# Wo's loads, a K halo and sums of h in another order, and two more groups whose MLP runs all 18 pairs of W2 rows in seven products

## The chip, the cores and the metric

The kernel runs on one core of a Trainium2 chip. The metric is the device time of one execution, in microseconds (us). A core has the engines PE (TensorE: matmuls, and weight loads beside them), DVE (VectorE), ACT (ScalarE), POOL (GpSimd) and SP (SyncE, which here only issues DMAs). Each engine runs its own instructions in order and waits on semaphores for the others. DMA queues move data between DRAM and the core's memory.

## The reference, cut to what matters

One transformer block on 2048 tokens with D = 576, 32 heads of 18, and an MLP width F = 4608. Attention is local and dilated: each token looks at 8 positions, itself and every second one before it.

```python
def _A_ref(x, wqkv, wo):                       # H=32, Dh=18, W=8, dil=2
    q, k, v = split(x @ wqkv)
    idx = pos[:, None] - arange(W)[None, :] * dil          # masked where negative
    logits = einsum("bhsd,bhswd->bhsw", q, k[:, :, idx]) * Dh ** -0.5
    o = einsum("bhsw,bhswd->bhsd", softmax(logits), v[:, :, idx])
    return o.reshape(B, S, D) @ wo

def _B_ref(x, w1, b1, w2, b2):
    h = _gelu(einsum("bsd,df->bsf", _layernorm(x), w1) + b1)
    return einsum("bsf,fd->bsd", h, w2) + b2

h  = x + _A_ref(_layernorm(x), A_wqkv, A_wo)
h2 = h + _B_ref(_layernorm(h), B_w1, B_b1, B_w2, B_b2)
```

## The kernel before

**Tiling.** The 2048 tokens are 16 tiles of 128 rows (one row of each 16 neighbours, so that tile j - 2 holds the neighbours that tile j looks at). x, q and the K and V of eight tiles (`kv_ring`, one ring for even and one for odd tiles) stay on the core. The weights are loaded once: Wo in four slices (`load_wo`, two DMAs each, line 104), W1 in six, W2 in seven. W2 has 36 row tiles of 128 rows, taken as 18 pairs of an even and an odd one.

**Order.** Every engine's instruction order is written by hand. First come 24 visits of q, k and v products (PE, line 222), each with work in the tables `between` and `after` and with weight loads in `loads`, all keyed by the number of the visit. The normalized x goes through DRAM and comes back transposed (`out_x` lines 284 and 285, `in_x` line 288, both issued by SP). The attention and second layer norm of the first two tiles are in these visits too.

Then a loop over 8 groups of two tiles. In iteration k PE does the first MLP product of group k (324 matmuls), the Wo products of group k + 1 (36 matmuls, `wo_visit`), and the second MLP product of group k. Beside it DVE does the attention logits of group k + 2 (`att_qk_a` line 344, `att_qk_b` lines 353 to 364, `att_max` lines 368 and 369), the softmax denominators and probabilities (`att_den`, lines 395 to 397), the weighted sums of V (lines 401 to 408), the residual `ln2_h` (line 467) and its statistics. ACT does the gelu (line 578), the exponentials and the normalizations; POOL does the inverse roots (lines 161 and 492) and the accumulating DMAs `accumulate_h` and `out_sum` (line 787).

**Queues around the change.** SP issues in order: the attention output goes to DRAM (`send_o`, lines 204 and 205, tile `td`) and is read back transposed (`read_o`, line 439, tile `oT`), which Wo's products of the next group use as weights. The normalized h goes the same way (`ln2_send`, then `ln2_in`, line 508, into the tile `hnT`, of which there is one buffer). The output stores are on SP too (line 790). A K or V halo (`halo`, line 339) reloads one ring slot behind the product that read it; its issue waits for that product. An issue that waits holds up all issues behind it on SP. `reload_x` (line 462) brings back x of a later group.

**The second MLP product.** Groups 0 and 1 run it plainly (line 597). From group 2 on, `mlp2_fast` takes two token tiles, the even and odd W2 rows and the two halves of the columns as a product of 2x2 blocks and computes it with seven block products in place of eight. For this DVE makes four sums of h for each pair of row tiles (`h_sums`, line 667) and four sums of W2 (`w2_sums`, line 657), the latter once. In the text of the sums S0 to S3 and T0 to T3 are the first index `t`. The sums of h of the first 12 pairs are made in operations of 128x1536, those of pairs 12 to 15 in 128x512, pairs 12 to 17 in 128x768. Groups 2 to 5 take 16 pairs in seven products and the last two pairs plainly (16 x 7 + 2 x 8 = 128 matmuls of 128x288), groups 6 and 7 take all 18 (126). `mlp2_fast` runs a list of steps: a pair (n, range) is product n, a name is a point at which the hooks of the loop are called ("hc", "h", "6", "7", "in", "exp", "4", "3"), or a step of its own.

Sums have no memory of their own; `s_slot` and `t_slot` place them in parts of `kv_ring`, `q_all` and `x_all` that are free at that time.

Of the kernel before, what the change touches and what calls it, by code (L numbers as in the profile page):

```python
# [11 lines left out]
BF16 = mybir.dt.bfloat16  # L12
F32 = mybir.dt.float32
F16 = mybir.dt.float16
# [3 lines left out]
def kernel(  # L18
# [13 lines left out]
    P = 128  # L32
# [6 lines left out]
    KT = 5  # L39
# [5 lines left out]
    HALF = D // 2  # L45
# [10 lines left out]
    GROUPS = [ATT_ORDER[i:i + 2] for i in range(0, NT, 2)]  # L56
# [551 lines left out]
    def ring_blocks(r, b0, n, size):  # L608
        flat = kv_ring[r][:].rearrange("p w t d -> p (w t d)").bitcast(F16)
        return flat[:, b0:b0 + n * size].rearrange("p (m c) -> p m c", c=size)  # L610
# [5 lines left out]
    def t_slot(t, m0, m1):  # L616
        if t == 2:
            return w2_block(0, 1, m0, m1).bitcast(F16)
        i = (0, 1, None, 2)[t]
        if m0 >= 16:  # L620
            return ring_blocks(1, (2 * i + m0 - 16) * HALF, m1 - m0, HALF)
        if i == 2 and m0 < 16:
            return ring_blocks(0, RING_T + m0 * HALF, m1 - m0, HALF)
        part = 0 if m1 <= 8 else 1 if m1 <= 12 else 2
        rows, j0 = ((x_all, (1, 9, 13)[part]), (q_all, (4, 12, 0)[part]))[i]
        m = m0 - (0, 8, 12)[part]
        j = j0 + 2 * (m // 2)
        if m1 - m0 > 2:
            return rows[:, j:j + m1 - m0 - 1:2, :].bitcast(F16).rearrange("p a (b c) -> p a b c", c=HALF)
        return rows[:, j, (m % 2) * HALF:(m % 2 + m1 - m0) * HALF].bitcast(F16).rearrange("p (b c) -> p b c", c=HALF)  # L630

    SR = 12
    ring1_free = [False]
    step_of = [0]
    RING_T = 3 * SR * P

    def s_slot(t, m0, m1):
        if t == 2:
            return h_block(0, 1, m0, m1)
        i = (0, 1, None, 2)[t]  # L640
        if m0 < SR:
            return ring_blocks(0, (i * SR + m0) * P, m1 - m0, P)
        if not ring1_free[0]:
            rows, j = ((q_all, 15), (x_all, 10), (x_all, 8))[i] if step_of[0] == 2 else (q_all, 15 - 2 * i)
            return rows[:, j, (m0 - SR) * P:(m1 - SR) * P].bitcast(F16).rearrange("p (m c) -> p m c", c=P)
        return ring_blocks(1, 6 * HALF + (i * (NM - SR) + m0 - SR) * P, m1 - m0, P)

    def h_block(odd, i, m0, m1):
        return h_all[:, 2 * m0 + odd:2 * m1:2, i * P:(i + 1) * P].bitcast(F16)
# [49 lines left out]
    def c_(fn, *a):  # L699
        return lambda: fn(*a)  # L700
# [2 lines left out]
        return ap.rearrange("p (g c) -> p g c", g=2)  # L703

    def mlp2_fast(g, rows, tags, wo, hooks):
        last, summed = wo is None, rows < NM
        q, p, r, s = tags
        j0, j1 = g
        af = psum_pair(q, "po")
        a, f = (af[:, n, 0:HALF] for n in range(2))  # L710
        b, d = psum_pair(p, "po")[:, 0, 0:HALF], None
        o0, o1 = (new_o(j, summed) for j in g)
        flat = kv_ring[1][:].rearrange("p w t d -> p (w t d)")
        rest = halves(flat[:, W * 2 * D - 2 * D:W * 2 * D].bitcast(F32))
        bank = {1: a, 2: a, 3: f, 4: b, 6: b}

        def add(out, x, y):
            nc.vector.tensor_tensor(out=out, in0=x, in1=y, op=ALU.add)

        def last_out():  # L720
            nc.vector.tensor_copy(out=o0[:, HALF:HALF + HALF // 2], in_=f[:, 0:HALF // 2])
            nc.scalar.copy(out=o0[:, HALF + HALF // 2:D], in_=f[:, HALF // 2:HALF])
            nc.sync.dma_start(out=out3[:, j0, HALF:D], in_=o0[:, HALF:D])

        def out0(n0, n1):
            if summed:
                nc.scalar.copy(out=halves(o0), in_=af[:, :, 0:HALF])
                return
            add(halves(o0)[:, n0:n1], af[:, n0:n1, 0:HALF], halves(x_of(j0))[:, n0:n1])
            nc.sync.dma_start(out=out3[:, j0, n0 * HALF:n1 * HALF], in_=o0[:, n0 * HALF:n1 * HALF])  # L730

        def out1():
            if summed:
                add(o1[:, HALF:D], bank[5], o1[:, 0:HALF])
                add(o1[:, 0:HALF], b, o1[:, 0:HALF])
                out_sum(j1)
                return
            add(o1[:, 0:HALF], b, rest[:, 0])
            add(o1[:, HALF:D], bank[5], rest[:, 1])
            nc.sync.dma_start(out=out3[:, j1, :], in_=o1)  # L740

        def do_rest():
            if summed:
                nc.scalar.copy(out=o1[:, 0:HALF], in_=bank[7])
                return
            add(rest, bank[7].unsqueeze(1).to_broadcast([P, 2, HALF]), halves(x_of(j1)))

        def take():
            bank[7], bank[5] = (psum_pair(tag, "po")[:, 0, 0:HALF] for tag in (r, s))

        lo, hi, all_ = (0, SR), (SR, rows), (0, rows)
        seed = {"b": (1, 6), "d": (6, 5), "f": (5, 3)}
        does = {
            "wo": lambda: wo((r, s)), "e": take, "rest": do_rest, "o1": out1,
            "o0": lambda: last_out() if last else out0(0, 2), "lo": lambda: out0(0, 1),
            "11": lambda: plain(0, 0, a, rows), "12": lambda: plain(0, 1, f, rows),
            "21": lambda: plain(1, 0, b, rows), "22": lambda: plain(1, 1, bank[5], rows),
        }
        if rows < NM:
            steps = ["wo", "hc", (1, all_), "b", "h", "e", (7, lo), (2, all_), (6, all_), "6", "7", "d", "11", (7, hi), "rest", "in",  # L760
                      (5, all_), "f", "exp", (4, all_), "21", "22", "o1", "4", (3, all_), "12", "o0", "3"]
        elif not last:
            steps = ["wo", "hc", (1, all_), "b", "h", "e", (7, lo), (6, all_), "6", "d", "7", (2, all_), (7, hi), "rest", "in",
                     (5, all_), "f", (4, all_), "o1", "4", (3, all_), "o0"]
        else:
            steps = ["e", (1, lo), (7, lo), (1, hi), "b", "h", (7, hi), "rest", (6, all_), "d", (2, all_), "lo",
                     (5, all_), "f", (4, all_), "o1", (3, all_), "o0"]
        for step in steps:
            if isinstance(step, tuple):
                product(step[0], bank[step[0]], *step[1])  # L770
            elif step == "f" and last:
                add(f, bank[5], x_of(j0)[:, HALF:D])
            elif step in seed:
                nc.scalar.copy(out=bank[seed[step][1]], in_=bank[seed[step][0]])
            else:
                call([does[step]] if step in does else hooks.get(step, ()))
# [22 lines left out]
    with tc.manual_schedule(engines={ENG.PE, ENG.Activation, ENG.DVE, ENG.SP, ENG.Pool}):  # L799
# [129 lines left out]
            ln2_ins(c, d)  # L929

        loads = {}
        for v, fns in ((2, [(load_w1, 0)]), (3, [(load_w1, 1)]), (4, [(load_w1, 2)]), (6, [(load_wo, [0])]), (8, [(load_wo, [1, 2])]),
                       (11, [(load_wo, [3])]), (14, [(load_w1, 4)]), (18, [(load_w1, 5), (load_w2, 0)]), (19, [(load_w2, 1)]),
                       (20, [(load_w2, 2)]), (21, [(load_w2, 3)]), (22, [(load_w2, 4)])):
            loads[v] = [c_(*fn) for fn in fns]
        after = {
# [87 lines left out]
        def wo_visit(*duos, fill=False):  # L1024
            visit([wo_duo(j, tag) for j, tag in duos], (lambda: [ahead[0]() for _ in range(2)]) if fill else None)

        FULL = (6, 7)
        p, q, r, s = "ABDC"

        gelu_table()  # L1030
        for k, g in enumerate(GROUPS):
# [38 lines left out]
            if 2 < k < 7:  # L1070
                m1[0] += [c_(pv_sum, c), c_(send_o, c), c_(pv_sum, d), c_(read_o, c), c_(send_o, d), c_(read_o, d)]
            if k < 6:
                m1[1] = m1.get(1, []) + [c_(att_qk_one, e, 0)]
                m1.setdefault(3, [])
                if k == 2:
                    m1[0] += [c_(pv_sum, d), c_(send_o, d), c_(read_o, d)]
                    m1[3] += [c_(w2_sums, 0, 8, (2, 3)), c_(w2_sums, 8, 12, (2, 3)), c_(w2_sums, 12, 14, (0, 1)), c_(w2_sums, 14, 16, (0, 1)),
                              c_(w2_sums, 12, 14, (2, 3)), c_(w2_sums, 14, 16, (2, 3))]
                m1[3] += [c_(h_sums, 0, SR, (0,))]
                x["hc"] += [c_(h_sums, 0, SR, (2,))]  # L1080
                x["h"] += [c_(h_sums, 0, SR, (1, 3)), c_(h_sums, SR, 16)]
                x["7"] += [c_(att_max, [e]), c_(att_qk_one, f, 1), c_(att_max, [f])]
                x["exp"] += [c_(exps, e, f)]
                x["4"] += [c_(att_den, e, f)]
            else:
                if k == 6:
                    ring1_free[0] = True
                    m1[1].append(c_(w2_sums, 16, NM))
                m1[3] = m1.get(3, []) + [c_(h_sums, 0, SR)]
                if k == 7:  # L1090
                    mid[3] = {1: [c_(h_sums, SR, 16)]}
                    x["h"] += [c_(h_sums, 16, NM)]
            if k + 3 < len(GROUPS):
                x["3" if k == 2 else "in"] += [c_(reload_x, GROUPS[k + 3])]
            wo = None
            if c is not None:
                if k == 6:
# [51 lines left out]
```

## Time and profile before

| what | value |
|---|---|
| median of 3 runs | 358.5 us (358.41 to 358.68) |
| the profiled execution | 358.75 us |
| its span | 357.0 us |
| granted TensorE clock | 1.00 |
| matmuls, busy time of PE | 4945, 351.1 us |
| busy time of DVE, ACT, POOL | 298.2, 235.9, 47.6 us |
| DMA moved | 46.29 MB |

How to read it: the profile gives one execution. The span runs from the first to the last instruction that it records; the profiled time holds 1.75 us more. A line of a timeline has the start, the duration, the engine ("SPq" is SP issuing DMAs), the line of the kernel, the operation with what it writes and reads, and in brackets how long the engine was idle before it and what ended that. A line of the chain of waits has start, duration, engine and what ran; each step is followed back to what released it. Matmul rows overlap, since matmuls are pipelined. A line of the queues has the packets, the megabytes and the share of the time of 16 DMA engines; q8 brings instructions.

### The profile page before, as it was taken

The numbers are of one execution on the slowest core, as the hardware profiler recorded it, in microseconds if no ns is written. First come the engines' busy times: TensorE is split into PE (matmuls) and PEld (weight loads), VectorE is DVE, ScalarE is ACT, GpSimd is POOL, SyncE is SP. The second block draws the span as 40 slices with busy tenths as digits, with TensorE's granted clock in tenths as the row PEclk, the third lists the DMA queues.
The fourth block names the chain that finished last, engine by engine and source line by source line (L and its number), as shares of the span: only waits on it lengthen the run. The fifth ranks groups of instructions, "written<-read, shape, count | busy, mean of one in ns | idle before, by whom it ended". The sixth has DMA issues, their size and how long they took to land.

```text
span 357.0 us, 11587 instructions
## 1 busy us (share of the span) xinstructions
PE 351.1 (98%) x4945; PEld 287.4 (81%) x4945; DVE 298.2 (84%) x428; ACT 235.9 (66%) x524; POOL 47.6 (13%) x63
## 2 busy tenths in 40 slices
PE   8999999999999999999999999999999999999996
PEld 4787778887788877887788778877887788778874
DVE  5999999999988999999998999999999998520431
ACT  4889767996647692678567856695669566606620
POOL 2340004000212010201200220022002200210000
PEclk9999999999999999999999999999999999999999
DMA  7997799954847574942553445345535353262001
GB/s 244 327 292 188 174 249 291 388 195 89 207 72 119 162 230 76 129 75 69 92 101 75 117 104 79 86 109 108 85 85 101 66 87 50 59 129 38 4 1 34
DMA packets 63492, 46.29 MB, mean 130 GB/s; under 512 B 32192, under 2 KB 61760, under 8 KB 63440
## 3 DMA queue, kind: packets, MB, share of 16 engines
q1 hardware_dynamic: 59472, 41.50, 44.1%
q0 software_dynamic: 3744, 3.84, 10.3%
q8 instruction: 38, 0.62, 0.7%
q10 hardware_dynamic: 224, 0.22, 0.2%
q14 instruction: 14, 0.11, 0.1%
HBM read 23.38 MB, written 12.42 MB: 100 GB/s over the span
## 4 chain that ended last, share of the span: by engine, by line
DVE 43%; PE 43%; DMA 6%; issue 3%; ACT 2%; SPq 2%; POOL 0%; DVEq 0%; POOLq 0%; ACTq 0%
PE po L687 21%; PE pm L222 19%; DVE prod L401 7%; DVE prod L353 7%; DVE prod L344 6%; DVE prod L407 5%; DVE ln_stats L148 3%; PE pw L222 2%; DMA kv_ring<-kv_dram 2%; DVE h L467 1%; DMA x_all<-in_A_x_dram 1%; DVE den L395 1%; ACT h_all L578 1%; DVE q_all L408 1%; DMA td<-q_all 1%
## 5 line engine op out<-in xcount | busy, mean ns | idle before, releaser
L222 PE MATMUL pm<-hnT,w_sb 64*128 64x256 bf16 x2304 | 142.9, 269 | 0.0
L578 ACT ACTIVATE h_all<-pm,b_sb 128x256 f16<-128x256 f32 (+1 forms) x288 | 108.5, 497 | 50.8 <-PE pm L222 50.2
L222 PEld LDWEIGHTS <-w_sb 64*128 64x128 bf16 x2304 | 111.6, 94 | 15.1 <-issue 1.7
L222 PE MATMUL pq<-wq_sb,xnT 64*128 64x288 bf16 x720 | 54.9, 283 | 1.2 <-DMA xnT<-xd 0.6
L687 PEld LDWEIGHTS <-h_all 128*128 128x128 f16 x464 | 44.8, 98 | 12.9 <-issue 1.4
L222 PEld LDWEIGHTS <-xnT 64*128 64x128 bf16 x864 | 41.9, 94 | 12.4 <-DMA xnT<-xd 0.9
L353 DVE TENSOR_TENSOR prod<-prod 128x2304 bf16<-128x2304 bf16 (+1 forms) x64 | 44.2, 691 | 2.1
L401 DVE TENSOR_TENSOR prod<-kv_ring,probs 128x4608 bf16<-128x4608 bf16 x16 | 40.9, 2558 | 1.9 <-DMA kv_ring<-kv_dram 1.4
L344 DVE TENSOR_TENSOR prod<-kv_ring,q_all 128x4608 bf16<-128x4608 bf16 x16 | 40.9, 2555 | 0.2
L222 PE MATMUL pm<-hnT,w1h_sb 64*128 64x256 bf16 x288 | 39.2, 269 | 0.0
L407 DVE TENSOR_TENSOR prod<-prod 128x2304 bf16<-128x2304 bf16 (+1 forms) x32 | 33.9, 1058 | 1.1
L597 PEld LDWEIGHTS <-h_all 128*128 128x128 bf16 x288 | 27.8, 98 | 8.0 <-issue 1.2
L687 PE MATMUL po<-w2a_sb,h_all 128*128 128x288 bf16 (+1 forms) x252 | 34.0, 286 | 0.0
L687 PEld LDWEIGHTS <-kv_ring 128*128 128x128 f16 x252 | 24.7, 98 | 6.2
L597 PE MATMUL po<-w2a_sb,h_all 128*128 128x288 bf16 x224 | 28.6, 286 | 0.0
L787 POOL DMA_DIRECT2D x_all<-o_sb x12 | 10.7, 889 | 126.4 <-PE pw L222 54.4
L222 PE MATMUL pq<-wqh_sb,xnT 64*128 64x288 bf16 x144 | 27.4, 283 | 0.0
L492 POOL TENSOR_TENSOR ln_rstd<-ln_var,mhalf 128x1 f32<-128x1 f32 x13 | 9.8, 758 | 77.7 <-ACT ln_var L491 77.7
L667 DVE TENSOR_TENSOR kv_ring<-h_all 128x1536 f16<-128x1536 f16 (+3 forms) x9 | 6.8, 754 | 15.7 <-ACT h_all L578 15.7
L222 PE MATMUL pw<-wo_sb,oT 64*128 64x288 bf16 x256 | 19.5, 283 | 0.1
L161 POOL TENSOR_TENSOR ln_rstd<-ln_veps,mhalf 128x1 f32<-128x1 f32 (+2 forms) x14 | 13.1, 947 | 44.3 <-PE o_pt L182 26.4
L687 PE MATMUL po<-w2b_sb,h_all 128*128 128x288 bf16 (+1 forms) x112 | 18.8, 286 | 0.1
(121 smaller groups left out, 409.3 us busy)
## 6 DMA issues: line engine op xcount, KB each, us to landing
w_sb<-in_B_w_dram SPq DMA_DIRECT2D x6, 768.0 KB, 7.7
kv_ring<-kv_dram SPq DMA_DIRECT2D x28, 144.0 KB, 2.3
kv_dram<-kv_ring SPq DMA_DIRECT2D x13, 288.0 KB, 3.3
w2a_sb<-in_B_w_dram SPq DMA_DIRECT2D x3, 1008.0 KB, 10.2
x_all<-in_B_b_dram SPq DMA_DIRECT2D x15, 144.0 KB, 4.1
td<-q_all SPq DMA_DIRECT2D x14, 144.0 KB, 1.8
td<-hn SPq DMA_DIRECT2D x14, 144.0 KB, 1.8
x_all<-h POOLq DMA_DIRECT2D x14, 144.0 KB, 4.8
```

Source lines behind the costliest of these rows:

```text
L148: nc.vector.bn_stats(out=stats[:, i, c, :], in_=src[:, c * HALF:(c + 1) * HALF])
L161: nc.gpsimd.tensor_tensor(out=rstd[:], in0=veps[:], in1=mhalf[:].to_broadcast([P, n]), op=ALU.pow)
L222: last = nc.tensor.matmul(duo["g"][r ^ swap][i], lhsT=lhsT, rhs=rhs, start=(swap == 0 and i == 0 and kt == 0), stop=(swap == 1 and kt == K ...
L344: ins = nc.vector.tensor_tensor(out=prod[:], in0=k_ring[j % 2], in1=q_all[:, j, :].unsqueeze(1) .to_broadcast([P, W, D]), op=ALU.mult).ins
L353: nc.vector.tensor_tensor(out=prod[:, :, o * H:o * H + n], in0=prod[:, :, a * H:a * H + n], in1=prod[:, :, c * H:c * H + n], op=ALU.add)
L401: nc.vector.tensor_tensor(out=prod[:].rearrange("p w (d h) -> p w d h", h=H), in0=v_ring[j % 2].rearrange("p w (d h) -> p w d h", h=H), in ...
L407: nc.vector.tensor_tensor(out=prod[:, 0:n, :], in0=prod[:, 0:n, :], in1=prod[:, n:2 * n, :], op=ALU.add)
L492: ins = nc.gpsimd.tensor_tensor(out=rstd[:], in0=var[:], in1=mhalf[:], op=ALU.pow).ins
L578: pace[0] = nc.scalar.activation(out=hT(grp)[:, f, 0:N], in_=ps[:, r, i * N:(i + 1) * N], func=ACT.Gelu_apprx_tanh, bias=b1_sb[:, f:f + 1] ...
L597: nc.tensor.matmul(banks[half], lhsT=hT(grp)[:, f, i * P:(i + 1) * P], rhs=w2_rows(f)[:, half * HALF:(half + 1) * HALF], start=(f == 0), s ...
L687: nc.tensor.matmul(bank, lhsT=l, rhs=r, start=start, stop=stop, skip_group_check=True)
L787: nc.gpsimd.dma_start(out=x_of(j), in_=o_of.pop(j), accum_op=ALU.add)
```

## The change

It has seven parts.

1. The slices of Wo are issued after visits 5 (two) and 11 (two), where they were issued after 6 (one), 8 (two) and 11 (one).
2. The reload of the K halo of tile e moves from inside its logits to the step "hc".
3. In groups 3, 4 and 5 the sum S2 of the first 12 pairs is made together with S0, ahead of `ln2_h`, where it was made behind the first `ln2_h`.
4. Groups 4 and 5 run all 18 pairs in seven products (`FULL`), with four more sums of h of 128x256 each. The output keeps the summed form (`summed`) in groups 2 to 5.
5. The sums of W2 of the last two pairs are made in group 3 (T0, T1, ahead of the exponentials) and group 4 (T2, T3), where they were made in group 6.
6. The sums get other places: those of W2 rows of `q_all`, some of h `x_all` and `q_all` by group (`homes`), and S1 of pairs 12 to 17 in groups 4 and 5 a new allocation of the tile `hnT` (`new_top`).
7. `reload_x` of groups 5, 6 and 7 moves from group 2's "3", group 3's and 4's "in" to group 3's "3", group 4's "3" and group 4's "in".

```diff
@@ -618,7 +618,7 @@
             return w2_block(0, 1, m0, m1).bitcast(F16)
         i = (0, 1, None, 2)[t]
         if m0 >= 16:
-            return ring_blocks(1, (2 * i + m0 - 16) * HALF, m1 - m0, HALF)
+            return q_all[:, 15 - 2 * i, (m0 - 16) * HALF:(m1 - 16) * HALF].bitcast(F16).rearrange("p (m c) -> p m c", c=HALF)
         if i == 2 and m0 < 16:
             return ring_blocks(0, RING_T + m0 * HALF, m1 - m0, HALF)
         part = 0 if m1 <= 8 else 1 if m1 <= 12 else 2
@@ -631,7 +631,9 @@
 
     SR = 12
     ring1_free = [False]
-    step_of = [0]
+    step_of, top = [0], [None]
+    homes = {2: ((q_all, 15), (x_all, 10), (x_all, 8)), 3: ((q_all, 11), (x_all, 10), (x_all, 8)),
+             4: ((q_all, 9), (x_all, 4), (x_all, 6)), 5: ((q_all, 9), (q_all, 5), (q_all, 7))}
     RING_T = 3 * SR * P
 
     def s_slot(t, m0, m1):
@@ -641,9 +643,16 @@
         if m0 < SR:
             return ring_blocks(0, (i * SR + m0) * P, m1 - m0, P)
         if not ring1_free[0]:
-            rows, j = ((q_all, 15), (x_all, 10), (x_all, 8))[i] if step_of[0] == 2 else (q_all, 15 - 2 * i)
-            return rows[:, j, (m0 - SR) * P:(m1 - SR) * P].bitcast(F16).rearrange("p (m c) -> p m c", c=P)
-        return ring_blocks(1, 6 * HALF + (i * (NM - SR) + m0 - SR) * P, m1 - m0, P)
+            if step_of[0] in FULL and t == 1:
+                rows, c = top[0][:].rearrange("p k c -> p (k c)"), 0
+            else:
+                rows, j = homes[step_of[0]][2 if m0 >= 16 else i]
+                rows, c = rows[:, j, :], (16 - SR - i) * P if m0 >= 16 else 0
+            return rows[:, (m0 - SR) * P - c:(m1 - SR) * P - c].bitcast(F16).rearrange("p (m c) -> p m c", c=P)
+        return ring_blocks(1, (i * (NM - SR) + m0 - SR) * P, m1 - m0, P)
+
+    def new_top():
+        top[0] = sb.tile([P, KT, 2 * P], BF16, tag="hnT", name="hnT")
 
     def h_block(odd, i, m0, m1):
         return h_all[:, 2 * m0 + odd:2 * m1:2, i * P:(i + 1) * P].bitcast(F16)
@@ -703,7 +712,7 @@
         return ap.rearrange("p (g c) -> p g c", g=2)
 
     def mlp2_fast(g, rows, tags, wo, hooks):
-        last, summed = wo is None, rows < NM
+        last, summed = wo is None, g not in GROUPS[6:]
         q, p, r, s = tags
         j0, j1 = g
         af = psum_pair(q, "po")
@@ -756,7 +765,7 @@
             "11": lambda: plain(0, 0, a, rows), "12": lambda: plain(0, 1, f, rows),
             "21": lambda: plain(1, 0, b, rows), "22": lambda: plain(1, 1, bank[5], rows),
         }
-        if rows < NM:
+        if summed:
             steps = ["wo", "hc", (1, all_), "b", "h", "e", (7, lo), (2, all_), (6, all_), "6", "7", "d", "11", (7, hi), "rest", "in",
                       (5, all_), "f", "exp", (4, all_), "21", "22", "o1", "4", (3, all_), "12", "o0", "3"]
         elif not last:
@@ -929,8 +938,8 @@
             ln2_ins(c, d)
 
         loads = {}
-        for v, fns in ((2, [(load_w1, 0)]), (3, [(load_w1, 1)]), (4, [(load_w1, 2)]), (6, [(load_wo, [0])]), (8, [(load_wo, [1, 2])]),
-                       (11, [(load_wo, [3])]), (14, [(load_w1, 4)]), (18, [(load_w1, 5), (load_w2, 0)]), (19, [(load_w2, 1)]),
+        for v, fns in ((2, [(load_w1, 0)]), (3, [(load_w1, 1)]), (4, [(load_w1, 2)]), (5, [(load_wo, [0, 1])]),
+                       (11, [(load_wo, [2, 3])]), (14, [(load_w1, 4)]), (18, [(load_w1, 5), (load_w2, 0)]), (19, [(load_w2, 1)]),
                        (20, [(load_w2, 2)]), (21, [(load_w2, 3)]), (22, [(load_w2, 4)])):
             loads[v] = [c_(*fn) for fn in fns]
         after = {
@@ -1024,7 +1033,7 @@
         def wo_visit(*duos, fill=False):
             visit([wo_duo(j, tag) for j, tag in duos], (lambda: [ahead[0]() for _ in range(2)]) if fill else None)
 
-        FULL = (6, 7)
+        FULL = (4, 5, 6, 7)
         p, q, r, s = "ABDC"
 
         gelu_table()
@@ -1070,28 +1079,37 @@
             if 2 < k < 7:
                 m1[0] += [c_(pv_sum, c), c_(send_o, c), c_(pv_sum, d), c_(read_o, c), c_(send_o, d), c_(read_o, d)]
             if k < 6:
-                m1[1] = m1.get(1, []) + [c_(att_qk_one, e, 0)]
+                m1[1] = m1.get(1, []) + [c_(att_qk_a, e), c_(att_qk_b, e, 0)]
+                x["hc"] += [c_(halo, e, 1)]
                 m1.setdefault(3, [])
                 if k == 2:
                     m1[0] += [c_(pv_sum, d), c_(send_o, d), c_(read_o, d)]
                     m1[3] += [c_(w2_sums, 0, 8, (2, 3)), c_(w2_sums, 8, 12, (2, 3)), c_(w2_sums, 12, 14, (0, 1)), c_(w2_sums, 14, 16, (0, 1)),
                               c_(w2_sums, 12, 14, (2, 3)), c_(w2_sums, 14, 16, (2, 3))]
-                m1[3] += [c_(h_sums, 0, SR, (0,))]
-                x["hc"] += [c_(h_sums, 0, SR, (2,))]
-                x["h"] += [c_(h_sums, 0, SR, (1, 3)), c_(h_sums, SR, 16)]
+                m1[3] += [c_(h_sums, 0, SR, (0,) if k == 2 else (0, 2))]
+                if k == 2:
+                    x["hc"] += [c_(h_sums, 0, SR, (2,))]
+                x["h"] += [c_(h_sums, 0, SR, (1, 3))]
+                if k in FULL:
+                    x["h"] += [new_top, c_(h_sums, SR, 16), c_(h_sums, 16, NM)] + [c_(w2_sums, 16, NM, (2, 3))] * (k == FULL[0])
+                else:
+                    x["h"] += [c_(h_sums, SR, 16)]
                 x["7"] += [c_(att_max, [e]), c_(att_qk_one, f, 1), c_(att_max, [f])]
+                if k == 3:
+                    x["exp"] += [c_(w2_sums, 16, NM, (0, 1))]
                 x["exp"] += [c_(exps, e, f)]
                 x["4"] += [c_(att_den, e, f)]
             else:
                 if k == 6:
                     ring1_free[0] = True
-                    m1[1].append(c_(w2_sums, 16, NM))
                 m1[3] = m1.get(3, []) + [c_(h_sums, 0, SR)]
                 if k == 7:
                     mid[3] = {1: [c_(h_sums, SR, 16)]}
                     x["h"] += [c_(h_sums, 16, NM)]
-            if k + 3 < len(GROUPS):
-                x["3" if k == 2 else "in"] += [c_(reload_x, GROUPS[k + 3])]
+            if k in (3, 4):
+                x["3"] += [c_(reload_x, GROUPS[k + 2])]
+            if k == 4:
+                x["in"] += [c_(reload_x, GROUPS[7])]
             wo = None
             if c is not None:
                 if k == 6:
```

## The prediction

> **What bounds the kernel now.** I read the busy table first, then the groups of PE's waits, then the chain of waits, then the timelines around the places that these name. The profiled execution took 358.75 us, of which the span is 357.0 us; 1.75 us lie outside it. The median of the runs shown is 358.5 us, so I work on 358.75 and take 0.25 off at the end.
>
> ```profile
> PE 351.1 (98%) x4945; PEld 287.4 (81%) x4945; DVE 298.2 (84%) x428; ACT 235.9 (66%) x524; POOL 47.6 (13%) x63
> ...
> q8 instruction: 38, 0.62, 0.7%
> ```
>
> PE is busy for 98% of the span. Only fewer matmuls or the few gaps can give time. Of PE's waits, the one in mid-kernel with a line of its own is this:
>
> ```profile
> PE pq L222 <- DMA xnT<-xd: 0.6, 1, 0.6
> ```
>
> The chain of waits runs on DVE until group 3, hands over to PE through the transfer of the attention output, and stays on PE for the rest:
>
> ```profile
> 187.92 0.47 DVE q_all L408
> ...
> 188.80 3.68 DMA td<-q_all
> ...
> 192.53 2.91 DMA oT<-td
> ...
> 195.49 1.77 PE pw L222 x26
> ...
> 197.25 15.79 PE po L687 x128
> ...
> 213.04 17.79 PE pm L222 x324
> ...
> 304.60 15.54 PE po L687 x126
> ```
>
> The reader is to see two regimes. Before 195.49 a gain of PE alone is lost again, because DVE decides when PE may start its Wo matmuls there (about 0.27 us of waiting). After it every matmul less is time less, as long as what DVE and the queues deliver is not late.
>
> **The matmuls.** Groups 4 and 5 go from 128 to 126 matmuls in the second MLP product. The chain shows 15.79 us for 128 and 15.54 us for 126: 0.25 us for each group, two groups, **-0.49 us** unrounded (4 x 15.79/128). They lie in the PE regime, so they count in full unless a wait takes them back.
>
> **Wo's loads.** PE waits at 42.37 for a transposed read that SP issued behind Wo's loads.
>
> ```profile
> 36.28 0.43 SPq L104 DMA_DIRECT2D woh_sb<-in_A_wo_dram  x1
> 36.82 1.53 SPq L288 DMA_TRANSPOSE xnT<-xd  x1
> ...
> 42.37 0.66 PE L222 MATMUL pq<-wq_sb,xnT 64*128 64x288 bf16 x8 [0.61 <-DMA xnT<-xd]
> ```
>
> Four Wo issues stand ahead of it, from 34.80 to 36.71, and its input had landed by 35.7. Without them it can go 1.1 us earlier, more than the gap (0.61 us in the view, 0.78 us from matmul start to matmul start), so this stall goes. Next is late what comes at 61:
>
> ```profile
> 60.60 0.73 POOL L161 TENSOR_TENSOR ln_rstd<-ln_veps,mhalf 128x1 f32<-128x1 f32 x1 [0.57 <-DVE ln_nmean L481]
> ```
>
> POOL's root waits for DVE, which runs back to back from 35 to 62; ACT's normalization, its copy of a q product at 62.47 and the first MLP matmuls stand behind that root. The matmul at 63.27 needs the bank that the copy frees at 63.10, 0.17 us earlier. So of 0.78 us at most 0.17 us is kept, and that reaches 195 only through DVE, which idles 0.70 us at 101 for ACT's exponentials. Ends 0 and -0.17; I take **-0.10**, the middle. The two issues added at visit 11 stand at 43 to 45, some 0.9 us ahead of the next two transposed reads (landed 47.64 and 55.72), for which PE comes 2.5 and 2.3 us after they have landed: hidden, and 0 unless they come over 2.3 us later. Wo is read first at 56.02.
>
> **The K halo** moves behind the output stores of group 1 in group 2 alone; elsewhere SP's order is as before, and DVE's work is the same. The halo's reader is a whole group later: 0.
>
> **DVE's sums.** In group 3 one sum of 128x1536 moves ahead of the wait for Wo. That wait is 1.48 us, so the 0.87 us are hidden there and gone behind it. Two new W2 sums stand ahead of the exponentials' denominators, at 0.45 us each: about -0.87 + 0.9 = 0. In group 4 the same sum goes into this wait:
>
> ```profile
> 232.59 0.76 DVE L467 TENSOR_TENSOR h<-pw,x_all 128x576 f32<-128x576 f32 x1 [1.08 <-PE pw L222]
> 233.26 0.95 DVE L667 TENSOR_TENSOR h_all<-h_all 128x1536 f16<-128x1536 f16 x1
> ...
> 237.45 0.42 DVE L667 TENSOR_TENSOR h_all<-h_all 128x512 f16<-128x512 f16 x1
> ```
>
> That is -0.87 (233.26 to 234.13). Added are four sums of 128x256: four of 128x512 take 1.46 us here (236.66 to 238.12), four of 128x768 take 2.00 us in group 6, so by the same step four of 128x256 take about 0.92. Added are two W2 sums: four take 1.81 us in group 6, so 0.90. Together **+0.95 us on DVE** in group 4. From 233.26 to 262.8 DVE has no idle time, so everything behind is 0.95 us later: a halo and the transposed read for the next MLP (needed 2.16 us after it landed, so hidden), then the attention output of group 6's second tile, whose last operation ends at 260.21. Its way to PE has no slack:
>
> ```profile
> 262.30 1.21 SPq L439 DMA_TRANSPOSE oT<-td  x1
> ...
> 266.94 0.28 PE L222 MATMUL pw<-woh_sb,oT 64*128 64x288 bf16 x2
> 267.06 0.65 PE L222 MATMUL pw<-wo_sb,oT 64*128 64x288 bf16 x8
> ```
>
> This read takes 4.65 us and lands at 266.95; PE's first weight load from it is at 267.00. In groups 4 and 6 the same read takes 2.78 us, so the duration decides. The DMA view of 264 to 267 shows what is beside it:
>
> ```profile
> q8 instruction: 1, 0.02, 1.9%
> ```
>
> One packet of instructions, issued 2.6 us into the read. In group 2 a read with such a packet 1.5 us after its issue took 4.06 us. After the change the issue comes at 263.25 and the packet, which goes by PE's progress, at about 264.8, 1.55 us behind: the row of group 2 is the nearest. It lands at 267.31. PE, 0.25 us earlier by group 4's two matmuls, wants it at 266.75: a **stall of 0.56 us**. Ends: at 2.78 us it lands at 266.03, no stall; at 4.65 us it lands at 267.90, 1.15 us.
>
> The Trainium skill, page "Runtime: NRT & Kernel Launch", section "Instruction fetch mechanics", says that the sequencer streams instructions in blocks over a queue of its own while it executes, and that crossing a block is mostly hidden. For the instruction stream itself the trace agrees: PE does not stop at the 38 packets. For a transfer beside one, the rows differ (4.65 against 2.78 us); by the rule alone this stall would be nothing, which is the first rival below.
>
> Group 5 adds four small sums as well (0.92 us) and hides one large one; its successors have 1.28 us (the transposed read of the MLP input) and 1.32 us (the next attention output) to spare, and group 6 loses 1.8 us of W2 sums ahead of an operation that waited 0.40 us for ACT: 0.
>
> **Homes and reloads.** The sums' new places, one of them a new allocation of the MLP input's tile, make that tile's next transposed read wait for the product that reads it; this product starts near 239 and the read was issued at 242.18: 0. The x reloads now land at 213 and 249 beside POOL's accumulating writes, just ahead of a K/V halo that DVE needs 0.28 us after it landed (254.69, 254.97). Ends 0 and +0.5 (a halo of the same size took 2.1 to 3.6 us here); I take 0.
>
> **Sum:** -0.49 - 0.10 + 0.56 = -0.03: 358.72, and 0.25 off: **358.5 us**.
>
> **Rivals.**
> - The read keeps its 2.78 us, because the packet misses it or slows it little. Then -0.49 - 0.10 = -0.59: 357.9. For it: two of three such reads in groups 4 to 6 took 2.78. Against: a packet falls into it by the count of instructions.
> - Faster: as the first, and the wait at 195.49 goes too. Its first transfer took 3.68 us against a median of 1.8, again with an instruction packet beside it; without it 0.27 us are won, and the early gain is the whole 0.17. -0.49 - 0.17 - 0.27 = -0.93: 357.6. Against: PE moves little ahead of 195, so the packet likely hits again.
> - Slower: DVE's lateness grows. The reload delays the halo by 0.5 us and the read takes 4.65: it lands at 263.25 + 0.5 + 4.65 = 268.40, a stall of 1.65 us: +1.16 without the early gain, 359.7. It decides from a landing after 267.96, where the stall passes 0.49 + 0.72. For it: no idle time on DVE for 29 us, and 0.28 us of spare.
> - The change doesn't do what it says: that can be excluded, since its instruction order has four matmuls fewer and the new sums in groups 3, 4 and 5.
>
> **How the numbers follow.** 0.2% is 0.72 us, about what a measurement can tell here. Chances: forecast 0.38, first rival 0.23, faster 0.22, slower 0.17. The range reaches from 357.5 to 359.3: it holds the forecast with both ends of its read (to 359.2), the first rival and nearly all of the faster case, and leaves out the slower one. Faster by over 0.2% is below 357.8: the faster case and 0.05 of the first rival's spread, 0.27. Slower is above 359.2: the slower case and 0.03 of the forecast, 0.20. The same: 0.53.
>
> **What would show it.** The wait for xnT near 42 gone from PE's waits; 126 matmuls and 15.54 us in groups 4 and 5; DVE's last attention operation ahead of group 5's Wo about 0.95 us later; the read oT issued near 263.2, an instruction packet beside it, PE's wait for it about 0.5 us. Wrong would be: no such wait, a wait of PE in the products of groups 4 and 5 for a sum, or early time that is kept past 195.

## The result

The changed kernel is slower: a median of 360.43 us (9 runs) against 358.54 us, a ratio of 1.0059 with the interval 1.0045 to 1.0072, or 1.6 to 2.6 us more. Its profiled execution took 360.0 us with a span of 358.2 us, 1.25 us more than that of before; it is the fastest of its nine, and one taken again later (359.71 us) is the fastest of six. So the profile explains 1.25 us; what other executions add to it no trace here shows. Two of the nine have a mean granted clock of 0.995 and took 361.93 and 362.98 us; both profiled executions have 1.00.

The busy times and the instruction packets:

```profile
PE 351.4 (98%) x4941; PEld 287.1 (80%) x4941; DVE 299.9 (84%) x436; ACT 235.9 (66%) x524; POOL 47.8 (13%) x63
...
q8 instruction: 38, 0.62, 0.7%
```

The four matmuls are gone, and DVE has 1.7 us more. PE's waits (in all, times, longest):

```profile
PE pw L222 <- ACT h_all L578: 1.1, 1, 1.1
...
PE pq L222 <- DMA xnT<-xd: 0.5, 1, 0.5
PE po L696 <- ACT po L783: 0.4, 1, 0.4
PE pw L222 <- DMA oT<-td: 0.3, 1, 0.3
```

The first is put down to ACT, which had long been done: the wait ended with the landing of a read, below. The second is at 50, the last at 195. Behind 200 two waits are new, and the chain of waits shows them:

```profile
269.52 0.76 DVE h L467
270.30 0.78 ACT hn L489 x2
...
272.21 0.40 ACT po L783
...
272.65 11.92 PE po L696 x96
...
304.09 1.77 PE pw L222 x26
305.85 15.54 PE po L696 x126
```

Measured from matmul start to matmul start, less the usual 0.12 us, they are 0.55 us (272.65) and 1.27 us (304.09). From the Wo products near 195 to the end of the span, to two decimals, the kernel before takes 356.97 - 195.49 = 161.48 us and the changed one 358.22 - 195.40 = 162.82: +1.34, which is -0.49 for the matmuls, +0.55 and +1.27, within 0.01.

**The wait at 304** is for the attention output of the last group, which SP and the DMA view show:

```profile
299.49 1.21 SPq L439 DMA_TRANSPOSE oT<-td  x1
```
```profile
DMA to landing us min/median/max: 4.6/4.6/4.6
```

Before, this read was issued at 298.62 and took 2.78 us, with 1.32 us to spare. Now it comes 0.87 us later and takes 1.77 us more. An instruction packet starts 2.54 us behind its issue; but one started 2.53 us behind it in the kernel before too, and did no harm. The DMA packets of the two traces show the difference. Before, the read's own packets (640 of 256 B and 32 of 4 B) had all ended 2.34 us behind the issue. Now the last four of them begin only as the instruction packet ends, 3.45 to 3.54 us behind the issue, and the read lands 1.0 us after them. Some 0.2 us decided between the two.

By these rows neither part makes the wait alone: 0.87 us late with a read of 2.78 us would leave 0.45 us to spare, and a read of 4.55 us issued as early as before would make 0.45 us of wait (both estimates).

**The wait at 272.** DVE's timeline of group 5, before and after (start, duration, idle time ahead of it in brackets):

```profile
266.40 0.88 DVE L667 TENSOR_TENSOR kv_ring<-h_all 128x1536 f16<-128x1536 f16 x1
268.37 0.76 DVE L467 TENSOR_TENSOR h<-pw,x_all 128x576 f32<-128x576 f32 x1 [1.09 <-PE pw L222]
```
```profile
267.72 0.88 DVE L676 TENSOR_TENSOR kv_ring<-h_all 128x1536 f16<-128x1536 f16 x1
268.64 0.96 DVE L676 TENSOR_TENSOR h_all<-h_all 128x1536 f16<-128x1536 f16 x1
269.52 1.41 DVE L467 TENSOR_TENSOR h<-pw,x_all 128x576 f32<-128x576 f32 x2
```

DVE reaches S0 1.32 us late, so the idle 1.09 us that was to hide S2 no longer exists, and the residual begins 1.15 us late. ACT normalizes it and only then copies the bank of product 1 (L783); product 2 may not overwrite that bank sooner. Behind the sums of group 4 DVE was 0.92 us late, and 0.81 us ahead of the weighted sums of V (250.51 against 249.70). The rest of the 1.32 us is a halo that landed late, for which DVE idles 0.55 us:

```profile
256.30 2.56 DVE L401 TENSOR_TENSOR prod<-kv_ring,probs 128x4608 bf16<-128x4608 bf16 x1 [0.55 <-DMA kv_ring<-kv_dram]
```

### The profile page after: what moved, and what is told of

Same layout as the page of the kernel before. It is cut to its first block, busy times and chain, and to the rows that moved or that the text cites. A ratio compares the mean times of both kernels' runs of the same rounds, so it can differ in the third digit from the quotient of the medians.

```text
span 358.2 us, 11597 instructions
## 1 busy us (share of the span) xinstructions
PE 351.4 (98%) x4941; PEld 287.1 (80%) x4941; DVE 299.9 (84%) x436; ACT 235.9 (66%) x524; POOL 47.8 (13%) x63
## 4 chain that ended last, share of the span: by engine, by line
PE 78%; DVE 10%; ACT 5%; DMA 4%; SPq 1%; issue 1%; DVEq 0%; ACTq 0%
PE pm L222 33%; PE po L696 20%; PE pq L222 12%; PE po L597 10%; ACT h_all L578 3%; PE pw L222 3%; DVE prod L353 2%; DVE prod L401 1%; DMA xnT<-xd 1%; DVE prod L344 1%; DMA x_all<-in_A_x_dram 1%; SPq L104 1%; DMA kv_ring<-kv_dram 1%; DVE ln_stats L148 1%; DMA oT<-td 1%
## 5 line engine op out<-in xcount | busy, mean ns | idle before, releaser
L696 PEld LDWEIGHTS <-h_all 128*128 128x128 f16 x448 | 43.2, 98 | 13.1 <-issue 2.0
L783 ACT COPY po<-po 128x288 f32<-128x288 f32 x17 | 6.5, 385 | 18.4 <-PE po L696 18.4
```

The source lines that it names most:

```text
L696: nc.tensor.matmul(bank, lhsT=l, rhs=r, start=start, stop=stop, skip_group_check=True)
```

## The experiments

Each was timed in five rounds beside the kernel before; times are medians. "272" and "304" are PE's waits there in its profile, from start to start less 0.12 us; the last column has its other waits over 0.3 us behind 190, without the 0.3 us near 342 that every kernel has, before too.

| kernel | us | ratio (interval) | 272 | 304 | others |
|---|---|---|---|---|---|
| changed, again | 360.64 | 1.0077 (1.0054 to 1.0099) | 0.19 | 0.97 | 0.40 at 196 |
| wo_back | 360.10 | 1.0048 (1.0028 to 1.0068) | 0.66 | 1.10 | 0.32 at 196 |
| s2_back | 362.22 | 1.0119 (1.0087 to 1.0152) | none | 1.16 | 0.33 at 196, 0.39 at 232 |
| full_back | 358.87 | 1.0023 (1.0005 to 1.0041) | none | none | none |
| wo_alone | 358.80 | 1.0010 (0.9990 to 1.0029) | none | none | none |
| s2_alone | 358.45 | 0.9999 (0.9986 to 1.0012) | none | none | none |
| late_alone | 358.39 | 0.9994 (0.9986 to 1.0003) | none | none | none |
| reload_alone | 358.40 | 0.9998 (0.9989 to 1.0006) | none | none | none |
| no_sums | 358.63 | 0.9999 (0.9991 to 1.0008) | none | none | 0.41 at 196 |
| nosums_wo | 358.41 | 0.9994 (0.9981 to 1.0007) | none | none | 0.37 at 196 |
| five_plain | 359.54 | 1.0038 (1.0020 to 1.0056) | 0.67 | none | none |
| four_plain | 359.39 | 1.0027 (1.0016 to 1.0038) | 0.13 | 0.65 | 0.31 at 196 |
| reload_mid | 359.71 | 1.0027 (1.0017 to 1.0037) | none | 1.31 | none |
| shift_late | 359.42 | 1.0026 (1.0015 to 1.0037) | none | none | 0.81 at 267 |
| mid_late | 358.95 | 1.0016 (1.0005 to 1.0028) | none | none | 0.73 at 267 |
| shift_early | 361.54 | 1.0072 (1.0045 to 1.0100) | 0.80 | 0.20 | none |
| pool_mid | 362.97 | 1.0126 (1.0103 to 1.0148) | none | none | 3.40 at 222 |
| pool_two | 362.22 | 1.0103 (1.0090 to 1.0116) | none | none | 0.84 at 232, 0.54 at 250, 1.96 at 270 |

**Parts of the change undone.** My theory after reading the traces: DVE's sums of groups 4 and 5 make both waits, and a packet lengthens the second. The rivals: Wo's loads, S2's place, the reloads of x.

```diff
-... (5, [(load_wo, [0, 1])]), (11, [(load_wo, [2, 3])]), ...           # wo_back
+... (6, [(load_wo, [0])]), (8, [(load_wo, [1, 2])]), ... (11, [(load_wo, [3])]), ...
-m1[3] += [c_(h_sums, 0, SR, (0,) if k == 2 else (0, 2))]      # s2_back
-if k == 2:
+m1[3] += [c_(h_sums, 0, SR, (0,))]
+if True:
     x["hc"] += [c_(h_sums, 0, SR, (2,))]
```

> The changed kernel with Wo's loads where they were before. Theory: the loss of the change lies behind 260, where DVE's sums of groups 4 and 5 make the attention output late (PE waits of 0.55 us at 272.65 and 1.27 us at 304.09 in its trace); the early part of the kernel is absorbed by DVE until 195. Then the time stays at the changed kernel's 360.4 us (360.0 to 360.7), the PE wait near 42 is back with 0.6 to 0.8 us, and the one at 50 (0.62 us in the changed kernel) is gone. Rival: the two issues added ahead of the transposed read at 44.8, which made PE wait at 50, cost the time: then it falls by 0.6 us or more, to 359.8 or less.

> The changed kernel with the sum S2 of the first 12 pairs behind the first residual again, in groups 3 to 5 as well. Theory: the wait of 0.55 us at 272.65 (ACT's copy of a bank stands behind the normalization of a residual that DVE began 1.15 us later than before, since S0 and S2 stand ahead of it) goes to 0.1 us or less, but the attention output of the last group is set by DVE, so PE waits that much longer for it near 304 (about 1.8 us in place of 1.27): total as the changed kernel, 360.4 us (360.0 to 360.8). Rival: the wait at 272.65 is a cost of its own: then the total falls by 0.5 us to 359.9 or below and the wait near 304 stays.

full_back leaves parts 4 to 7 of the change out.

> The kernel before with the Wo loads, the K halo and the sum S2 as in the changed kernel, but with groups 4 and 5 as before (16 pairs in seven products, places of the sums and reloads of x as before). Theory: the whole loss comes with the 18 pairs of groups 4 and 5: this kernel takes 358.5 us (358.1 to 358.8), within 0.1% of the kernel before, and its trace shows no PE wait over 0.3 us behind 200, apart from a transposed read that meets a packet of instructions. Rival: the reordering itself costs (S2 ahead of the residual, or Wo): 359.0 us or more.

The changed kernel timed again has both waits again, smaller (0.19 and 0.97 us). wo_back stayed slow, and its two late waits stayed; early on, the wait near 42 was back (0.51 us) and the one at 50 gone. full_back lost the late waits and most of the time (its interval still lies above 1). So most of the loss comes with parts 4 to 7. In s2_back the wait at 272 went, as either side said, and the one at 304 was 1.16 us, not 1.8; its total was above all that was expected. What its other executions did is not shown.

**Each part alone** (from the kernel before; late_alone repeats one large sum of group 4):

```diff
-x["h"] += [c_(h_sums, 0, SR, (1, 3)), c_(h_sums, SR, 16)]     # late_alone
+x["h"] += [c_(h_sums, 0, SR, (1,))] * (k == 4) + [c_(h_sums, 0, SR, (1, 3)), c_(h_sums, SR, 16)]
```

> The kernel before with one large sum of group 4 (S1 of 12 pairs, 0.87 us of DVE) made twice, and nothing else: the lateness of the change without its matmuls, reloads and places. Theory: from 233 on DVE has no spare time, so the attention output is 0.87 us later at 263; its read is issued at 263.2, with a packet about 1.7 us behind, lands at 267.2 to 267.9, and PE, which wants it at 267.0, waits 0.2 to 0.9 us; nothing is won, so 358.7 to 359.4 us. Rival: DVE has spare time somewhere between and takes the lateness up: 358.5 us and no PE wait near 267.

> The kernel before with the reloads of x for the groups 5, 6 and 7 at the places of the changed kernel, and nothing else. Theory: the V halo of group 5 comes about 0.4 us late and DVE with it, and this alone costs as little as the sum of 0.87 us made twice did (358.39 us): 358.3 to 358.9 us. Rival: the reloads carry the 0.7 us (the difference of the changed kernel and reload_mid) by themselves: 359.2 us.

> The kernel before with Wo's loads at the changed kernel's places, and nothing else. If the loads cost the 0.3 us that no_sums lacks: 358.8 us or more, with a PE wait near 50 of 0.5 us or more and the wait near 195 of 0.3 us or more. If they are absorbed, as the prediction had it: 358.4 to 358.6 us.

> The kernel before with S2 and the K halo at the changed kernel's places, and nothing else. If the loads of Wo were the cost in full_back: 358.4 to 358.6 us, as before. If the reordering of S2 and the halo costs: 358.8 us or more, in some executions at least.

None of them alone costs anything that these runs can tell. But wo_alone has a wait of 0.71 us at 50 and lies just at the 358.8 us that was set for a cost of Wo's loads. In four pairs that differ by Wo's loads alone (wo_alone and before, full_back and s2_alone, no_sums and nosums_wo, changed and wo_back) the median is 0.2 to 0.5 us higher with the loads moved. No pair is clear of its noise, so a cost of that size is neither shown nor excluded. late_alone speaks against my forecast: its read for group 5 was late as said, but a packet 0.6 us into it made it 3.44 us, PE did not wait, and group 5's idle time took the 0.87 us up. Nor did reload_alone make the halo late (2.26 us, and DVE does not wait for it).

The late halo does not need DVE's added work either: no_sums, below, has it too (3.57 us, DVE idles 1.01 us). What the changed kernel has and reload_alone lacks are the new places of the sums. The x of group 6 goes to parts 4 and 6 of `x_all`, and part 6 holds sums of group 4 in the changed kernel. So SP waits with this load for products that read them, the last near 248.2:

```profile
SPq L462 <- PE po L696: 1.8, 1, 1.8
```

Thus the load stands at 248.5 to 249.3, beside POOL's accumulating writes (248.51 to 249.64); in reload_alone all four were issued by 245.98, ahead of POOL's first write at 246.95. In 14 of the 16 traces that record its landing, this halo lands 0.36 to 0.42 us behind the last of these writes. That write began 0.80 us later than before and took 6.19 us in place of 5.48, and the halo landed 1.52 us later. This is read from the traces; no run changed the places alone. The price is in the combination.

**Both groups are needed.**

```diff
-FULL = (4, 5, 6, 7)
+FULL = (4, 6, 7)      # five_plain
+FULL = (5, 6, 7)      # four_plain
```

> The changed kernel with group 5 on 16 pairs again (its plain products of the last two pairs read one block of W2 that holds a sum by then). Theory: the wait near 304 needs the sums of both groups. DVE's idle time ahead of the residual in each group (about 1.1 us before) is taken by S2 (0.87 us) in both; what group 4 adds (0.95 us, and 0.44 us from the late halo) eats that idle time in group 5, so S2 is no longer hidden there and the four small sums of group 5 come on top. Without them DVE is 0.9 us earlier at the last attention output, and the wait near 304 goes to 0.3 us or less; the one near 272 stays (0.3 to 0.6 us). 358.9 to 359.6 us. Rival: the lateness of group 4 alone makes the wait near 304: 360.4 us or more.

> The changed kernel with group 4 on 16 pairs again; T2 and T3 are then made in group 5. Theory: group 4 adds nothing on DVE, so the residual of group 5 is in time and the wait near 272 goes; group 5 adds 0.92 + 0.9 us (four sums of h, two of W2) and hides S2, so DVE is 0.95 us late at the last attention output, its read is met by a packet, and the wait near 304 stays (0.9 to 1.3 us). 359.2 to 360.2 us. Rival: the wait near 304 comes from group 4: it goes, and the time is 358.3 to 358.9 us.

```profile
PE po L696 <- ACT po L783: 0.5, 1, 0.5
```

That is five_plain: the copy's wait is there, the one near 304 is gone; DVE ends the last attention output 1.34 us earlier than in the changed kernel and then idles 2.66 us, in place of 1.22, ahead of the last sums:

```profile
298.81 0.96 DVE L676 TENSOR_TENSOR kv_ring<-h_all 128x1536 f16<-128x1536 f16 x1 [2.66 <-ACT h_all L578]
```

four_plain has 0.13 and 0.65 us. It looks like the mirror image, but its DVE is as late in group 5 as that of the changed kernel, without the sums of group 4, since it waits longer for the halo:

```profile
256.40 2.56 DVE L401 TENSOR_TENSOR prod<-kv_ring,probs 128x4608 bf16<-128x4608 bf16 x1 [1.25 <-DMA kv_ring<-kv_dram]
```

It reaches S0 at 267.83 (changed: 267.72), and ACT's copy ends at 272.70 (272.60). The wait is shorter because PE comes 0.52 us later, 0.25 of it the two matmuls that it has more in group 4. So the sums of group 5, on top of the lateness that it inherits, make the wait at 304 (in four_plain T2 and T3 are among them). The wait at 272 needs S2 ahead of the residual (s2_back) and the late halo (reload_mid, below); what the sums of group 4 add to it apart from the halo is not shown.

**DVE's work taken away** and **the packets moved**:

> The changed kernel, with the two W2 sums of group 4 and three of the four 128x256 sums of h in groups 4 and 5 left out (so the products of the last two pairs there use stale numbers; the matmuls are as in the changed kernel). Theory: DVE's work is the loss. DVE is 1.6 us earlier in group 4 than in the changed kernel and 0.7 more in group 5, the waits at 272.65 (0.55 us) and 304.09 (1.27 us) go, 358.0 to 358.6 us in all: the matmuls' gain of 0.49 us can be seen at last, unless a packet of instructions meets a read. Rival: the loss comes from the new places of the sums or from the reloads of x (DMA traffic), not from DVE's work: 359.5 us or more, with the waits in their places.

> no_sums (the changed kernel without the two W2 sums of group 4 and three of the four small sums of h in groups 4 and 5, so on stale numbers) with Wo's loads back at their old places. If Wo's loads cost 0.3 to 0.5 us early: 358.0 to 358.3 us, so that the matmuls' gain shows. Rival: the gain is lost behind 200, in executions other than the profiled one: 358.6 us again.

> The changed kernel with 36 PE instructions fewer in the warm-up at the start (18 matmuls with their weight loads, whose results nothing reads; the warm-up's PE time stays about the same). The packets of instructions come each 256 PE instructions, so all of them move 36 instructions, about 1 us, later against the work. Theory: a packet that falls into a transposed read makes it 1.3 to 1.9 us longer. In the changed kernel one comes 2.5 us into the read oT for the last group (4.55 us) and one 0.3 us into that for the group ahead (2.8 us). Moved, the first comes behind its read (2.8 us, the PE wait near 304 falls from 1.27 us to 0.3 us or less) and the second 1.3 us or more into its read (3.5 to 4.7 us, a PE wait near 267 of 0.3 to 1.3 us). Total 359.3 to 360.4 us. Rival: the packets do nothing and DVE's lateness alone makes the waits: then the read for the last group takes 4.5 us again, the waits stay where they are, and the total stays at 360.4 us.

> The changed kernel with 150 more PE instructions in the warm-up (shorter ones, in about the same time; their results are read by nothing), so that all packets of instructions come 150 instructions, about 4 us, earlier against the work. Theory of the packets: in the groups 5 and 6 they then fall between the transfers of the attention output; the read for the last group takes 2.8 us, the PE wait near 304 goes to 0.1 us or less, the wait at 272.65 (0.55 us, DVE's lateness) stays: 358.6 to 359.3 us, plus what the warm-up delays the start. Rival: the packets do nothing: 360.4 us, with 1.27 us of wait near 304.

Without the sums both waits go, though places, reloads and matmuls are those of the changed kernel. From 196.07 the trace of no_sums needs 160.98 us, 0.50 less than before: the matmuls' gain, in the profile. In the medians it is not seen (358.63 us; with Wo's loads back 358.41, whose interval holds -0.14% as well as nothing); where it goes stays open.

shift_late moved the wait as the packets' theory said:

```profile
267.37 0.66 PE L222 MATMUL pw<-wo_sb,oT 64*128 64x288 bf16 x8 [0.65 <-DMA oT<-td]
```

The read for the last group took 2.9 us, with the same lateness (issued at 299.39), that for the group ahead 3.9, where the changed kernel has 4.55 and 2.8. shift_early cut the wait at 304 to 0.20 us too (the read took 2.9 us), but the wait at 272 was 0.80 us and its start was late; its total cannot be told from the changed kernel's by these intervals. The Trainium skill, page "Runtime: NRT & Kernel Launch", section "Instruction fetch mechanics", calls the crossing of a block mostly hidden. For PE the traces agree: it stops at none of the 38 packets. A transfer beside a packet is another matter, as these reads show.

**Reloads, and the sums on POOL.**

> The changed kernel with the reload of x for group 6 moved behind the V halo that it stood ahead of (SP issues it near 253.5 in place of 248.5). In the changed kernel that halo took 3.1 us in place of 2.4, and DVE waited 0.4 us for it at 256. Theory: the reload beside POOL's accumulating writes makes that halo late; the halo takes 2.1 to 2.5 us again, DVE is 0.4 us earlier from 256 on, and each of the PE waits at 272.65 and 304.09 shrinks by up to 0.4 us: 359.6 to 360.2 us. Rival: the halo was late for another reason (POOL's writes alone, which ended 1.5 us later): then it takes 3.1 us again and nothing moves, 360.4 us.

> The kernel with the later reload and, as in shift_late, 36 PE instructions fewer in the warm-up. If the two terms add, the read for the last group is not met by a packet (2.8 us, wait near 304 of 0.3 us or less), the one for the group ahead is met but was issued 0.4 us earlier (wait near 267 of 0.4 us in place of 0.81): 358.5 to 359.0 us, against 359.7 with the later reload alone and 359.4 with the shift alone. Rival: the two act on the same wait, and the time stays at 359.4 to 359.7 us.

> The kernel with the later reload (label reload_mid), and the four W2 sums of the last two pairs made by POOL in place of DVE (T0 and T1 in group 3, T2 and T3 at the start of group 4). Theory: DVE is then 0.9 us earlier in group 3 and 0.9 us earlier in group 4, the attention output of the last two groups comes in time, the PE wait near 304 (1.31 us there) falls to 0.4 us or less even when a packet of instructions meets its read, and the matmuls' 0.49 us show: 358.0 to 358.7 us. Rival: POOL's sums slow DVE's operations beside them or hold up POOL's accumulating writes, and nothing is won: 359.5 us or more.

> As pool_mid (later reload, W2 sums of the last two pairs on POOL), with T3 and T2 behind the two roots of the layer norm in group 4, so that PE does not wait for POOL at the start of that group (3.4 us there). Theory: DVE's added work was the loss; with 1.8 us of it on POOL no PE wait over 0.5 us is left behind 196, and the gain of 0.49 us of matmuls shows: 357.8 to 358.5 us. Rival: T2 comes too late for product 7, or the second root behind T3 makes the normalized h late: a PE wait near 243 or 249 of 0.5 us or more, 358.8 us or more.

reload_mid took the 0.55 us of idle time at 256 and the wait at 272 away, with the sums of group 4 in place: POOL's last write took 4.95 us, and S0 of group 5 began at 267.25. It won 0.3% on the changed kernel; with the packets moved as well, mid_late is the best version with 18 pairs in groups 4 and 5, and still slower than before. The sums on POOL cost more than on DVE. pool_mid made PE wait 3.4 us at a marker, an empty instruction on POOL that PE's next products wait for. In pool_two DVE stood still while POOL ran, first POOL's timeline and then DVE's:

```profile
237.50 1.52 POOL L666 TENSOR_TENSOR q_all<-w2b_sb,q_all 128x576 f16<-128x576 bf16 x1
...
239.69 1.28 POOL L666 TENSOR_TENSOR w2b_sb<-w2b_sb 128x576 f16<-128x576 bf16 x1
```
```profile
237.81 1.50 DVE L676 TENSOR_TENSOR h_all<-h_all 128x512 f16<-128x512 f16 x1
...
239.74 1.37 DVE L676 TENSOR_TENSOR x_all<-h_all 128x256 f16<-128x256 f16 x1
```

The same sums take 0.42 and 0.29 us alone: each lost 1.08 us, most of the 1.2 us in which POOL ran beside it.

## Why the prediction was wrong

The sum on record was -0.49 - 0.10 + 0.56 = -0.03 us; the profile has -0.49 - 0.09 + 0 + 0.55 + 1.27 = +1.24.

- **The matmuls**: right, 15.54 us for the 126 of each group.
- **Wo's loads**: the wait at 42 went, and a wait of 0.62 us at 50 came in its place: the next read was issued at 44.81 and took 5.13 us where 3.54 had been counted on, so it was not hidden. The amount kept at 195 was 0.09 us all the same.
- **DVE in group 4**: +0.95 said, +0.92 measured (240.01 against 239.09).
- **The read at 263**: no wait, where 0.56 us were forecast. It was issued at 263.52, but its packet came 0.3 us behind it, not 1.55, and it took 2.80 us: the first rival's case. The packet started 163 PE instructions past a multiple of 256, where it was 213 before; that is within the scatter of these packets (last section), so this miss was luck.
- **The step that failed** is "Group 5 adds four small sums as well (0.92 us) and hides one large one; its successors have 1.28 us ... and 1.32 us ... to spare ... : 0". It priced group 5 as if group 4 had left its idle time whole. With 1.32 us of lateness S2 was on the path: ACT's bank copy made 0.55 us of wait, and this copy stood in no step of the prediction. The 1.32 us to spare at the next attention output was counted with a read of 2.78 us; I had weighed a packet for the read at 263 only, not for this one, though the trace of the kernel before has a packet 2.53 us behind its issue. Here 0.87 us of lateness and 1.77 us more of read, less the time to spare, gave 1.27 us of wait.
- **Homes and reloads**: taken as 0 with an end of +0.5; the halo took 3.1 us and DVE waited 0.55 us. The two were priced one by one. Together, the load of group 6's x waits for products that read sums from its place, and so runs beside POOL's writes.
- The slower rival had the mechanism, DVE's lateness growing through the halo until a read of 4.65 us lands late, at the wrong read. I gave it 0.17, and left it outside the range.

That DVE's added sums are needed for the loss is shown by no_sums, and for the wait at 304 by five_plain; that the wait at 272 needs the late halo and S2's place by reload_mid and s2_back; that the packet sets the size at 304 by shift_late. Not settled: why the changed kernel's medians lie 0.4 us and more above its profiled executions, whether Wo's loads cost 0.2 to 0.5 us of that, and s2_back's total.

## What to carry to other kernels

Idle time that hides one move is spent once: when an edit is repeated over groups, carry the lateness of the first into the slack of the second before that slack is used again. Price a wait by the whole queue behind the late instruction, here an ACT copy that no dependency ties to the edit. A new place for a buffer is also a new wait for the load that fills this place next: look at both edits together. And where a critical transfer's duration has two values in the trace, put both into every later place where it is critical.

## What the runs showed of the hardware

The 95 transposed reads oT issued between 215 and 306 us in these 20 traces each have 640 DMA packets of 256 B. Undisturbed, the last of them ends 2.2 to 2.7 us behind the issue and the read takes 2.7 to 3.2 us. What an instruction packet adds goes by when it starts:

| instruction packet behind the issue | reads | the read took, us |
|---|---|---|
| 0 to 0.7 us | 26 | 2.8 to 3.6 |
| 0.8 to 2.2 us | 9 | 3.35 to 4.4, broadly longer the later the packet |
| 2.3 to 2.65 us | 6 | 4.4 to 4.65 |
| 2.3 to 2.65 us | 10 | 2.7 to 2.9 |

The other 44 reads had no instruction packet in this time, or one later than 2.7 us. The packets of the reads themselves tell the last two rows apart. In the ten, all of the read's packets had ended 2.42 us behind the issue, at most 0.06 us after the instruction packet had started. In the six, the last few of them, two of 4 B in one case, began only as the instruction packet ended, and the read landed 1.0 us or more after them. Why these last packets were some 0.2 us later is not shown. One read of shift_early, with a packet 0.1 us ahead of it, took 3.96 us: its own packets began 2.34 us behind the issue, elsewhere 1.3 to 1.5. The instruction packets come about each 256 PE instructions, with a scatter of some 50; that is 1.4 us in a group's first product (648 instructions in 17.79 us) and 3.1 us in the second (252 in 15.54).

A POOL sum of two operands and a DVE operation of two operands exclude each other in these traces: 0.42 us became 1.50 us, and a 128x4608 product in pool_two took 3.62 instead of 2.55 us. The Trainium skill, page "SBUF — State Buffer", section "Who interferes with whom", says that a DVE instruction with two inputs there contends with a POOL instruction that reads it, the later one blocking; the trace agrees.
